# Sparse attention and a sentence-level mixture of experts on one core: program order from a list scheduler, v loaded in 96 overlapping rows, evacuations on either engine

## The chip, the core and the metric

The kernel runs on one NeuronCore of a Trainium2 chip. TensorE (PE in the profile; PEld is its weight load), VectorE (DVE), ScalarE (ACT) and GpSimd (POOL) each run their own instructions in order and wait for each other by semaphores; SyncE (SP) issues the output stores. The metric is the device time of one execution in microseconds, the median of several runs.

## What is computed

Four batch elements, each in two stages: attention over 768 positions with 8 heads of 64, then one expert out of eight, chosen for the whole element.

```python
block, window = (32, 16)
k_sum = k.reshape(B, H, nb, block, D).max(axis=3)
v_sum = v.reshape(B, H, nb, block, D).mean(axis=3)
scores_l = scale * q @ k.T          # kept where |i - j| < window, else -1e9
scores_s = scale * q @ k_sum.T + log(block)
a = softmax(concat([scores_l, scores_s]))
x = a @ concat([v, v_sum])          # heads side by side: [B, 768, 512]
...
logits = x.mean(axis=1) @ w_gate    # one row of 8 for each element
e = argmax(logits)
out = softmax(logits)[e] * (relu(x @ w1[e]) @ w2[e])   # w1: 512 x 1024, w2: 1024 x 512
```

So each query sees the 31 positions around it and 24 block summaries.

## The kernel before

**Attention tiles.** Heads go in pairs (`pr`, four of them), queries in 12 blocks of 64 (`QB`), six blocks (`u`, 0 or 1) to a score tile. A query block needs 64 own keys, 16 on each side (the halo) and 24 summaries: 120 rows. `kaugs` holds these for k, transposed, and `vblks` for v, by rows. In both the own 64 rows come first, then 16 before, 16 behind, then 24 summaries. Batch elements use two of each in turn.

**Steps of a batch element.** `T_k` and `T_q` transpose one pair of k or q (16 transposes, L252) into PSUM; `copy_on` (L261 on ACT, L263 on DVE) puts them into `kaug` and `qT`. For k the engine is fixed by batch and pair, for q it is ACT. `K_rest` takes the block maximum (`kmx`, L282, read from PSUM) and fills the halos and summaries of `kaug` (L288, L291, L294), all on DVE. `S_tile` adds the mask by matmuls (L357), then the scores (L369), and ACT takes the exp (L379). `V_sum` (L307) sums v by blocks with the matrix `bind`, `V_copy` (L322) spreads the sums over `vblk`. `O_tile` (L393) multiplies by v and DVE divides by the row sum (L401, L404). `X_tile` transposes the result (L420) and ACT writes `xT` with its sum over positions (L421). `gate` (L434 to L474) computes the logits, reads the chosen expert into a GpSimd register and issues the six weight loads (L460, L463).

**Steps of the expert.** `H_chunk`: four matmuls of 384 columns (L498), relu on DVE where `ft` and `u` are odd, else on ACT (L507, L509). `O_chunk`: half of an output tile, four matmuls of 512 columns (L521); after the second half the tile is scaled by ACT or DVE in turn (L536, L531) and stored by SP (L537).

**What sets the order.** Program order is written out by hand and each engine keeps it. `a0` lists batch 0's attention pair by pair. Then `scores(1)` runs, and from there `weave` puts scores and values of batch b+1 between H and O chunks of batch b. GpSimd's queue holds all loads: batch 0's k and q by pairs with three v loads (64 own rows L104, halos L115 and L121) behind each, index patterns for the masks in between, then batch 1, and each later batch behind the weights of an earlier one. `warm` puts matmuls on a zero tile (`zb`, L240): nine of 512 columns at the start and two of 384 before the first score tile and the first output tile of each pair of batch 0.

**PSUM.** `sc` has two buffers of two banks for scores, `one` four of one bank for everything else.

Of the kernel before, what the change touches and what calls it, by code (L numbers as in the profile page):

```python
# [18 lines left out]
AX = mybir.AxisListType  # L19


@with_exitstack
def kernel(
# [23 lines left out]
    R_PRE = QB  # L47
    R_POST = QB + HALO
# [17 lines left out]
    ld = ctx.enter_context(tc.tile_pool(name="ld", bufs=3))  # L66
    work = ctx.enter_context(tc.tile_pool(name="work", bufs=3))
    apool = ctx.enter_context(tc.tile_pool(name="ap", bufs=9))
    small = ctx.enter_context(tc.tile_pool(name="small", bufs=3))
# [4 lines left out]
    sc_pool = ctx.enter_context(tc.tile_pool(name="sc", bufs=2, space=bass.MemoryType.PSUM))  # L74
    one_pool = ctx.enter_context(tc.tile_pool(name="one", bufs=4, space=bass.MemoryType.PSUM))
# [20 lines left out]
    def load_k(b, h0=0, h1=H):  # L96
        load_rows(b, "k", k, h0, h1)

    def load_q(b, h0=0, h1=H):
        load_rows(b, "q", q, h0, h1)  # L100

    def load_v(b, h0, h1):
        vb = vblks[b % NV]
        nc.gpsimd.dma_start(  # L104
            vb[0:QB, h0:h1, :, 0:D].rearrange("p h j d -> p (h j) d"),
            v[b, h0:h1].rearrange("h (j p) d -> p (h j) d", p=QB),
        )

    def load_halos(b, h0=0, h1=H):

        vb = vblks[b % NV].rearrange("p h j d -> p (h j) d")
        rows = v[b].rearrange("h s d -> (h s) d")
        n0, n1 = h0 * NJ, h1 * NJ
        a, z = max(n0, 1), min(n1, H * NJ - 1)
        nc.gpsimd.dma_start(  # L115
            vb[R_PRE : R_PRE + HALO, a:n1, 0:D],
            rows[(a - 1) * QB : (n1 - 1) * QB].rearrange("(n p) d -> p n d", p=QB)[
                QB - HALO : QB
            ],
        )  # L120
        nc.gpsimd.dma_start(  # L121
            vb[R_POST : R_POST + HALO, n0:z, 0:D],
            rows[(n0 + 1) * QB : (z + 1) * QB].rearrange("(n p) d -> p n d", p=QB)[
                0:HALO
            ],
        )

    def load_vp(b, pr):
        load_v(b, 2 * pr, 2 * pr + 2)
        load_halos(b, 2 * pr, 2 * pr + 2)  # L130

    def clear_ends(i, eng):

        eng.memset(vblks[i][QB:R_SUM, 0:1, 0:1, 0:D], 0.0)
        eng.memset(vblks[i][QB:R_SUM, H - 1 : H, NJ - 1 : NJ, 0:D], 0.0)
# [4 lines left out]
    load_k(0, 0, 2)  # L140
    clear_ends(0, nc.vector)
    identb = const.tile([128, 128], BF16, name="identb")
    make_identity(nc, identb)
    load_q(0, 0, 2)
    load_k(0, 2, 4)
    load_q(0, 2, 4)
    load_vp(0, 0)
    it_b = const.tile([QB, NJ, BLK], I32, name="it_b")
    nc.gpsimd.iota(it_b, pattern=[[-2, NJ], [1, BLK]], base=0, channel_multiplier=0)
    it_p = const.tile([128, 1], I32, name="it_p")  # L150
    nc.gpsimd.iota(it_p, pattern=[[0, 1]], base=0, channel_multiplier=1)

    it_m = const.tile([128, R_SUM], I32, name="it_m")
    nc.gpsimd.iota(it_m[:, 0:R_PRE], pattern=[[1, QB]], base=0, channel_multiplier=-1)
    nc.gpsimd.iota(
        it_m[:, R_PRE:R_POST], pattern=[[1, HALO]], base=-HALO, channel_multiplier=-1
    )
    nc.gpsimd.iota(
        it_m[:, R_POST:R_SUM], pattern=[[1, HALO]], base=QB, channel_multiplier=-1
    )  # L160
    load_vp(0, 1)
    load_k(0, 4, 6)
    load_q(0, 4, 6)
    load_vp(0, 2)
    load_k(0, 6, 8)
    load_q(0, 6, 8)
    load_vp(0, 3)

    def load_vs(b):
        load_v(b, 0, 4)  # L170
        load_v(b, 4, 8)
        load_halos(b)

    def load_all(b):
        load_k(b)
        load_q(b)
        load_vs(b)

    wg_sb = const.tile([128, NDT, E], FP32, name="wg_sb")
    nc.sync.dma_start(wg_sb, moe_w_gate.rearrange("(g p) e -> p g e", p=128))  # L180

    def edges(i, eng):

        eng.memset(vblks[i][0:QB, :, :, D:DP], 1.0)
        eng.memset(vblks[i][R_SUM:NR, :, :, D:DP], float(BLK))
        eng.memset(vblks[i][QB:R_SUM, :, :, D:DP], 1.0)
        eng.memset(kaugs[i][:, :, 0:1, R_PRE:R_POST], 0.0)
        eng.memset(kaugs[i][:, :, NJ - 1 : NJ, R_POST:R_SUM], 0.0)
        eng.memset(kaugs[i][:, :, :, NR:128], 0.0)

    edges(0, nc.vector)
    ones_row = const.tile([1, 128], FP32, name="ones_row")
    nc.vector.memset(ones_row, 1.0)
    ident6 = const.tile([128, NW, QB], BF16, name="ident6")
    for hh in range(2):
        rs = slice(hh * D, (hh + 1) * D)
        nc.vector.tensor_copy(
            ident6[rs], identb[rs, rs].unsqueeze(1).to_broadcast([QB, NW, QB])
        )
    pf = const.tile([128, 1], FP32, name="pf")  # L200
    nc.vector.tensor_copy(pf, it_p)
    half_id = const.tile([QB, 1], FP32, name="half_id")
    nc.vector.tensor_scalar(
        out=half_id, in0=pf[0:QB, :], scalar1=float(BLK), scalar2=None, op0=ALU.is_ge
    )
    bind = const.tile([QB, NJ, BLK], BF16, name="bind")
    nc.vector.tensor_scalar(
        out=bind, in0=it_b, scalar1=half_id[:, 0:1], scalar2=None, op0=ALU.is_equal
    )
    hi64 = const.tile([128, 1], FP32, name="hi64")  # L210
    nc.vector.tensor_scalar(
        out=hi64, in0=pf, scalar1=float(QB), scalar2=float(QB),
        op0=ALU.is_ge, op1=ALU.mult,
    )
    d_f = const.tile([128, R_SUM], FP32, name="d_f")
    nc.vector.tensor_scalar(
        out=d_f, in0=it_m, scalar1=hi64[:, 0:1], scalar2=None, op0=ALU.add
    )
    nc.vector.tensor_tensor(out=d_f, in0=d_f, in1=d_f, op=ALU.mult)

    mbias = const.tile([128, 128], BF16, name="mbias")
    nc.vector.memset(mbias[:, R_SUM:128], 0.0)
    nc.vector.tensor_scalar(
        out=mbias[:, 0:R_SUM], in0=d_f, scalar1=float(HALO * HALO), scalar2=OFF,
        op0=ALU.is_ge, op1=ALU.mult,
    )


    ends = []
    for i, c0 in enumerate((R_PRE, R_POST)):  # L230
        t = const.tile([128, 128], BF16, name=f"mb_end{i}")
        nc.vector.tensor_copy(t, mbias)
        nc.vector.memset(t[:, c0 : c0 + HALO], OFF)
        ends.append(t)

    def warm(ps, n, cols=384):


        for _ in range(n):
            nc.tensor.matmul(  # L240
                ps[:, 0:cols], lhsT=zb[:, 0:128], rhs=zb[:, 0:cols], start=True, stop=True
            )


    xT, red, qTs, xss, aTs = {}, {}, {}, {}, {}

    def transpose_pair(b, which, pr, name):
        src = nat[which, b]
        ps = one_pool.tile([128, RR, PR], BF16, name=name, tag="one")
        for r in range(RR):  # L250
            for hh in range(2):
                nc.tensor.transpose(  # L252
                    ps[hh * D : (hh + 1) * D, r, :],
# [24 lines left out]
    def K_rest(b, pr):  # L278
        def f():
# [16 lines left out]
            )  # L296
        return f

    vss = {}

    def V_sum(b, prs):
        def f():
# [357 lines left out]
```

## Time and profile before

| | |
|---|---|
| three runs | 182.45, 183.06, 184.3 us; median 183.06 |
| profiled execution | 183.01 us, its span 181.4 us |
| mean granted TensorE clock | 0.925 |
| data read from HBM, written | 38.78 MB, 6.29 MB |

The span is the time from the first to the last instruction of the profiled execution; the rest of its time lies around it. The columns of a group are its line, engine, operation and tiles, the count, the busy time and mean length of one, and the idle time of the engine just before it with what ended most of it:

```profile
L379 ACT ACTIVATE aT<-sc 128x768 bf16<-128x768 f32 x32 | 25.4, 813 | 15.7 <-PE sc L369 15.7
L509 ACT ACTIVATE hT<-hps 128x384 bf16<-128x384 f32 x48 | 23.7, 493 | 17.7 <-PE hps L498 17.2
L421 ACT ACTIVATE xT<-xps 128x384 bf16<-128x384 bf16 x32 | 15.6, 492 | 11.1 <-PE xps L420 10.4
L404 DVE TENSOR_TENSOR xs<-ops,rv 128x384 bf16<-128x384 f32 x32 | 17.8, 557 | 1.1
L282 DVE TENSOR_REDUCE kmx<-kps 128x24 bf16<-128x768 bf16 x16 | 15.2, 948 | 4.9 <-ACT kaug L261 4.8
L104 POOL DMA_DIRECT2D vblk<-in_v_dram x10 | 12.3, 1235 | 1.0 <-DMA vblk<-in_v_dram 1.0
```

On DVE and ACT the last figure is large where the engine waits for PE. A mean can mix forms: a v load of L104 lasted from 968 to 1414 ns on POOL, by its rows. The loads by number, KB of each and median us from issue to landing:

```profile
w_sb<-in_moe_w_dram POOLq DMA_DIRECT2D x12, 512.0 KB, 12.4
k_nat<-in_k_dram POOLq DMA_DIRECT2D x3, 768.0 KB, 14.9
vblk<-in_v_dram POOLq DMA_DIRECT2D x6, 384.0 KB, 21.5
w_sb<-in_moe_w_dram POOLq DMA_DIRECT2D x8, 128.0 KB, 5.0
```

### The profile page before, as it was taken

To read this page: it belongs to the slowest core of one execution; us is meant where nothing else is said; L and a number is where in the kernel's file an instruction comes from. 1 tells how busy PE (TensorE), PEld (TensorE's weight loads), DVE (VectorE), ACT (ScalarE), POOL (GpSimd) and SP (SyncE) were. 2 spreads that over 40 slices of the span, in tenths; PEclk is the share of its full clock that TensorE was granted. 3 is DMA by queue.
4 is the path that set the end of the run, shared out by engine and by line. 5 is a ranking of instruction groups with operands and counts; after the bars stand their busy time and mean duration, and the time that the engine had idled before them with its cause. 6 is when DMAs were issued, how large, how long until landed. Compare 5 with 4: busy or idle time off the path is not lost.

```text
span 181.4 us, 5192 instructions
## 1 busy us (share of the span) xinstructions
PE 159.2 (88%) x2229; PEld 93.8 (52%) x2241; DVE 90.9 (50%) x241; ACT 91.5 (50%) x187; POOL 53.4 (29%) x81
## 2 busy tenths in 40 slices
PE   7467997669996978999998999999979999999990
PEld 2245765447653554455554564455646544565440
DVE  4345476766417753476638752686287522122111
ACT  2243388457972743366663762666736821454120
POOL 7979980038910003982000007200000054000000
PEclk9855579975699999999999999999999999999999
DMA  4999999999999999999999996999400019995232
GB/s 46 143 159 155 125 185 192 128 90 135 196 198 208 167 125 65 110 232 252 235 231 182 126 61 86 148 234 255 102 0 4 0 16 181 260 260 98 87 144 116
DMA packets 60166, 26.02 MB, mean 143 GB/s; under 512 B 42736, under 2 KB 57072, under 8 KB 60144
## 3 DMA queue, kind: packets, MB, share of 16 engines
q0 software_dynamic: 56160, 19.39, 145.5%
q1 hardware_dynamic: 3984, 6.31, 10.1%
q8 instruction: 17, 0.28, 0.8%
q14 instruction: 5, 0.04, 0.1%
HBM read 38.78 MB, written 6.29 MB: 249 GB/s over the span
## 4 chain that ended last, share of the span: by engine, by line
PE 76%; DVE 12%; ACT 4%; POOL 3%; issue 3%; POOLq 0%; DVEq 0%
PE o_ps L521 23%; PE hps L498 22%; PE ops L393 5%; PE sc L369 4%; PE sc L357 4%; PE kps L252 4%; PE qps L252 4%; PE vsps L307 3%; PE xps L420 3%; DVE vblk L322 2%; DVE xs L404 2%; ACT xT L421 2%; DVE kmx L282 2%; PE ops L240 1%; ACT kaug L261 1%
## 5 line engine op out<-in xcount | busy, mean ns | idle before, releaser
L498 PE MATMUL hps<-xT,w_sb 128*128 128x384 bf16 x256 | 48.8, 328 | 0.0
L521 PE MATMUL o_ps<-w_sb,hT 128*128 128x512 bf16 x180 | 42.5, 380 | 1.5 <-issue 1.3
L460 POOL DMA_DIRECT2D w_sb<-in_moe_w_dram x16 | 12.1, 765 | 91.3 <-DVE gcol L484 58.4
L379 ACT ACTIVATE aT<-sc 128x768 bf16<-128x768 f32 x32 | 25.4, 813 | 15.7 <-PE sc L369 15.7
L509 ACT ACTIVATE hT<-hps 128x384 bf16<-128x384 f32 x48 | 23.7, 493 | 17.7 <-PE hps L498 17.2
L498 PEld LDWEIGHTS <-w_sb 128*128 128x128 bf16 x256 | 22.4, 98 | 13.1 <-issue 0.2
L521 PEld LDWEIGHTS <-hT 128*128 128x128 bf16 x192 | 17.3, 98 | 19.3
L531 DVE TENSOR_SCALAR o_sb<-o_ps,gcol 128x512 f32<-128x512 f32 x12 | 9.0, 751 | 25.2 <-PE o_ps L521 22.3
L421 ACT ACTIVATE xT<-xps 128x384 bf16<-128x384 bf16 x32 | 15.6, 492 | 11.1 <-PE xps L420 10.4
L404 DVE TENSOR_TENSOR xs<-ops,rv 128x384 bf16<-128x384 f32 x32 | 17.8, 557 | 1.1
L507 DVE TENSOR_SCALAR hT<-hps 128x384 bf16<-128x384 f32 x16 | 8.9, 558 | 18.0 <-PE hps L498 17.1
L282 DVE TENSOR_REDUCE kmx<-kps 128x24 bf16<-128x768 bf16 x16 | 15.2, 948 | 4.9 <-ACT kaug L261 4.8
L536 ACT ACTIVATE o_sb<-o_ps,gcol 128x512 f32<-128x512 f32 x12 | 8.3, 688 | 18.4 <-PE o_ps L521 18.3
L261 ACT COPY qT<-qps 128x768 bf16<-128x768 bf16 x16 | 12.8, 797 | 8.1 <-PE qps L252 8.0
L369 PE MATMUL sc<-qT,kaug 64*128 64x64 bf16 x384 | 12.5, 203 | 4.3 <-DVE kaug L294 4.3
L393 PEld LDWEIGHTS <-aT 120*64 120x64 bf16 x384 | 8.9, 113 | 13.5 <-DVE vblk L322 7.1
L393 PE MATMUL ops<-vblk,aT 120*64 120x65 bf16 x384 | 11.5, 201 | 4.8 <-DVE vblk L322 4.7
L369 PEld LDWEIGHTS <-kaug 64*128 64x128 bf16 x384 | 9.3, 104 | 7.4 <-issue 4.4
L263 DVE COPY kaug<-kps 128x768 bf16<-128x768 bf16 x10 | 9.5, 951 | 6.2 <-PE kps L252 6.2
L104 POOL DMA_DIRECT2D vblk<-in_v_dram x10 | 12.3, 1235 | 1.0 <-DMA vblk<-in_v_dram 1.0
L252 PE MATMUL qps<-identb,q_nat 96*64 96x96 bf16 x256 | 10.4, 236 | 2.0 <-DMA q_nat<-in_q_dram 2.0
L401 DVE RECIPROCAL rv<-ops 128x6 f32<-128x6 f32 x32 | 6.2, 193 | 11.9 <-PE ops L393 11.9
(81 smaller groups left out, 178.1 us busy)
## 6 DMA issues: line engine op xcount, KB each, us to landing
w_sb<-in_moe_w_dram POOLq DMA_DIRECT2D x12, 512.0 KB, 12.4
out_dram<-o_sb SPq DMA_DIRECT2D x24, 256.0 KB, 6.0
k_nat<-in_k_dram POOLq DMA_DIRECT2D x3, 768.0 KB, 14.9
q_nat<-in_q_dram POOLq DMA_DIRECT2D x3, 768.0 KB, 17.6
vblk<-in_v_dram POOLq DMA_DIRECT2D x6, 384.0 KB, 21.5
vblk<-in_v_dram POOLq DMA_DIRECT2D x6, 190.0 KB, 24.2
w_sb<-in_moe_w_dram POOLq DMA_DIRECT2D x8, 128.0 KB, 5.0
w_sb<-in_moe_w_dram POOLq DMA_DIRECT2D x4, 256.0 KB, 6.7
```

Of the source, the lines that this page charges most:

```text
L104: nc.gpsimd.dma_start(vb[0:QB, h0:h1, :, 0:D].rearrange("p h j d -> p (h j) d"), v[b, h0:h1].rearrange("h (j p) d -> p (h j) d", p=QB),)
L252: nc.tensor.transpose(ps[hh * D : (hh + 1) * D, r, :], src[:, 2 * pr + hh, r * D : (r + 1) * D], identb[0:PR, 0:PR],)
L261: nc.scalar.copy(out_, in_)
L282: nc.vector.tensor_reduce(out=kmx, in_=kpss.pop((b, pr)).rearrange("q r (n p) -> q n r p", n=NB), axis=AX.XY, op=ALU.max,)
L369: nc.tensor.matmul(sc[:, hh, w * QB : (w + 1) * QB], lhsT=ka[rs, pr, j, :], rhs=qT[rs, j * QB : (j + 1) * QB], start=False, stop=w == NW - ...
L379: nc.scalar.activation(aT, sc[:, :, 0:HB], ACT.Exp, scale=SCALE)
L393: nc.tensor.matmul(ops[w * QB : (w + 1) * QB, t, hh, :], lhsT=aT[0:NR, hh, c0 : c0 + QB], rhs=vb[0:NR, 2 * pr + hh, u * NW + 2 * t + w, 0 ...
L404: nc.vector.tensor_tensor(out=xs, in0=ops[:, :, :, 0:D], in1=rv.unsqueeze(3).to_broadcast([128, NW // 2, 2, D]), op=ALU.mult,)
L421: nc.scalar.activation(xT[b][:, pr, u * HB : (u + 1) * HB], xps, ACT.Copy, accum_out=red[b][:, pr, u : u + 1],)
L498: nc.tensor.matmul(hps[:, 0:HB], lhsT=w1_sb[:, dt, ft * 128 : (ft + 1) * 128], rhs=xT[b][:, dt, u * HB : (u + 1) * HB], start=(dt == 0), s ...
L509: nc.scalar.activation(dst, hps[:, 0:HB], ACT.Relu)
L521: nc.tensor.matmul(o_ps, lhsT=hTs[b][:, ft, st * 128 : (st + 1) * 128], rhs=w2_sb[:, ft, :], start=(ft == 0), stop=(ft == NFT - 1),)
```

## The change

Four things change together.

1. **Order.** The hand-written lists, `weave` and `run` go. Every step is split into its TensorE part and its evacuation, each becomes an `Op` with an engine, a duration, a priority, what it depends on and the PSUM or SBUF slot it takes. `Plan.solve` places them one by one: of the operations that could start within 0.03 us of the earliest, the one with the lowest priority number. The program is emitted in that order. The durations and hand-over times are constants in the code; TensorE's are taken 1.8 times as long before 24 us.
2. **Engine of an evacuation.** K and q copies, relu, output scaling and the block sums of v go to whichever of ACT and DVE would end them first in the plan. Exp and `xT` stay on ACT; `kmx`, halos, division and `V_copy` on DVE.
3. **v.** `vblk` and `kaug` now have the halo before, the own 64 rows, the halo behind in that order, so that a block's 96 rows are consecutive rows of v. One load fetches them for four heads at once, overlapping rows twice; the first block of batch 0 and the last of batch 3 have their own smaller load. `bind` has 96 rows, with zeros for the halo rows.
4. **Buffers and fillers.** `sc` has one buffer, `one` six; `ld` two, `work` and `small` four. `kmx` is read from `kaug` (SBUF), not from PSUM. Of the matmuls on `zb` only the nine at the start remain. V_sum of batch 0 runs twice for two pairs instead of four times for one.

```diff
+    def solve(self):
...
+            for op in left:
+                if any(d.end is None for d in op.deps):
+                    continue
+                r = max([d.end + self.LAT[d.eng] for d in op.deps], default=0.0)
...
+                for s in op.takes:
+                    h = hist[s.pool]
+                    if len(h) >= self.bufs[s.pool]:
+                        old = h[-self.bufs[s.pool]]
...
+                        r = max(r, max(u.end + self.LAT[u.eng] for u in old.users))
...
+                for eng, dur in op.engs:
+                    st = max(r, free.get(eng, 0.0))
+                    if eng == "pe" and st < self.slow_until:
+                        dur *= self.slow
+                    c = (st + dur, st, eng)
+                    if best is None or c < best:
+                        best = c
...
+            st, _, _, end, eng, op = min(
+                (c for c in found if c[0] <= smin + 0.03), key=lambda c: (c[1], c[2])
+            )
...
-    sc_pool = ctx.enter_context(tc.tile_pool(name="sc", bufs=2, space=bass.MemoryType.PSUM))
-    one_pool = ctx.enter_context(tc.tile_pool(name="one", bufs=4, space=bass.MemoryType.PSUM))
+    sc_pool = ctx.enter_context(tc.tile_pool(name="sc", bufs=1, space=bass.MemoryType.PSUM))
+    one_pool = ctx.enter_context(tc.tile_pool(name="one", bufs=6, space=bass.MemoryType.PSUM))
...
     def load_v(b, h0, h1):
-        vb = vblks[b % NV]
-        nc.gpsimd.dma_start(
-            vb[0:QB, h0:h1, :, 0:D].rearrange("p h j d -> p (h j) d"),
-            v[b, h0:h1].rearrange("h (j p) d -> p (h j) d", p=QB),
-        )
...
+        def cells(n0, n1, p0, p1):
+            nc.gpsimd.dma_start(
+                vb[p0:p1, n0:n1, 0:D],
+                bass.AP(
+                    v.tensor,
+                    v.offset + ((b * H * NJ + n0) * QB - HALO + p0) * D,
+                    [[D, p1 - p0], [QB * D, n1 - n0], [1, D]],
+                ),
+            )
...
+    def K_max(b, pr):
+        def f(eng):
+            kmxs[b, pr] = small.tile([128, NB], BF16, name="kmx")
+            nc.vector.tensor_reduce(
+                out=kmxs[b, pr].rearrange("q (j c) -> q j c", c=QB // BLK),
+                in_=kaugs[b % 2][:, pr, :, R_OWN:R_POST].rearrange(
+                    "q j (c t) -> q j c t", t=BLK
+                ),
...
-            if b == 0 and u == 0:
-                warm(sc[:, 0], 2)
...
-            if b == 0 and u == 0:
-                warm(ops.rearrange("p t h c -> p (t h c)"), 2)
...
+    plan = Plan(
+        {"one": 6, "sc": 1, "aT": 9, "qT": 4, "xs": 4, "hT": 2, "xT": 2, "o_sb": 4,
+         "w": 2},
+        slow_until=24.0, slow=1.8,
+    )
+    EITHER = lambda a, d: [("act", a), ("dve", d)]
...
+            own = add(EITHER(0.86, 1.0), K_own(b, pr), w, [tk] + wk)
+            kmx = add(("dve", 1.0), K_max(b, pr), w, [own])
+            rest = add(("dve", 0.6), K_rest(b, pr), w - 1, [own, kmx, R["edge", b % 2]])
...
+                s = R["S", b, pr, u] = add(
+                    ("pe", 0.4), S_mm(b, pr, u), w - 10, [rest, qo, R["mask"]], [ss])
+                e = R["e", b, pr, u] = add(
+                    ("act", 0.87), S_exp(b, pr, u), w - 10, [s], [at])
...
+                m = add(("pe", 0.66), H_mm(b, ft, u), base + ft,
+                        [R["w1", b, ft]] + [R["x", b, p, u] for p in ALLP], [sl])
+                o = add(EITHER(0.55, 0.6), H_out(b, ft, u), base - 165, [m],
...
+    ORDER = ["kq1", "v1", "w0", "kq2", "v2", "w1", "kq3", "v3", "w2", "w3"]
+    loads_kq(0, "k", [0], 0.8, KQ)
+    R["ident"] = add(("pool", 1.7), constants, 0, [last[0]])
...
+    for pr in ALLP:
+        if pr:
+            loads_kq(0, "k", [pr], 0.7, KQ)
+        loads_kq(0, "q", [pr], 0.7, KQ)
+        if pr == 1:
+            loads_v(0, [0, 1], 2.2, VV)
+    loads_v(0, [2, 3], 2.2, VV)
...
+    plan.solve()
+    plan.emit()
```

The order that the plan emits, where it differs most (each name a step for one pair; the number in front is the batch):

- Batch 0's k and q of the first two pairs are transposed first, then come the score tiles. Before batch 0's gate, TensorE also has all eight transposed pairs of batch 1 and its first two score tiles. After the gate come four more score tiles with V_sum of batch 1 among them, then the first w1 chunk of batch 0, six output tiles of batch 1 in a row, its last two score tiles and its `xT` transposes, and then the other w1 chunks.
- The eight transposed pairs of batch 2 stand within and behind batch 0's w1 chunks, its score tiles between batch 0's output halves. Batch 3 has the same places in batch 1.
- Output tiles of the expert come in twos: first half of both, then second half of both.
- GpSimd: k of pair 0, `identb`, three index patterns, q of pair 0, k and q of pair 1, v of pairs 0 and 1 (two loads), k and q of pairs 2 and 3, v of pairs 2 and 3, then batch 1 as before with two v loads.
- ScalarE gets nearly all relu and output scaling of the expert.

## The prediction

> **What bounds the kernel now.** I read the page first, then the busy time by stretches of the span, then TensorE's timeline and the list of waits. The page:
>
> ```profile
> span 181.4 us, 5192 instructions
> ...
> PE 159.2 (88%) x2229; PEld 93.8 (52%) x2241; DVE 90.9 (50%) x241; ACT 91.5 (50%) x187; POOL 53.4 (29%) x81
> ...
> PE   7467997669996978999998999999979999999990
> ...
> PEclk9855579975699999999999999999999999999999
> ...
> PE 76%; DVE 12%; ACT 4%; POOL 3%; issue 3%; POOLq 0%; DVEq 0%
> ```
>
> TensorE (PE) is busy 88% and is 76% of the chain that ended last; ScalarE and VectorE are at 50%. The digits say that this isn't one regime: PE reaches 9 and stays there only from the middle of the span, and PEclk has two holes on the left. Cut at those places (columns: length, then busy us and instruction count of PE, PEld, DVE, ACT, POOL, then granted clock, DMA share, GB/s):
>
> ```profile
> 8.00:24.80 16.80, 14.41 (x210) 9.79 (x210) 8.95 (x30) 7.55 (x12) 14.98 (x26) 0.50 1.69 149
> 24.80:38.40 13.60, 10.36 (x266) 7.53 (x264) 8.94 (x27) 8.43 (x22) 1.55 (x2) 1.00 2.93 159
> 38.40:48.60 10.20, 9.21 (x188) 7.00 (x182) 6.73 (x18) 8.05 (x11) 8.61 (x10) 0.50 2.43 140
> 48.60:70.78 22.18, 18.83 (x297) 11.33 (x296) 11.38 (x34) 12.82 (x34) 2.03 (x3) 1.00 2.70 162
> 41.90:45.30 3.40, 3.40 (x72) 2.62 (x70) 1.73 (x2) 2.62 (x5) 2.73 (x5) 0.50 1.75 152
> ```
>
> ```profile
> 70.78:108.25 37.47, 35.41 (x550) 20.38 (x555) 22.73 (x52) 20.90 (x43) 10.59 (x12) 1.00 2.15 176
> 108.25:145.52 37.27, 35.24 (x551) 20.39 (x556) 22.20 (x56) 21.29 (x45) 4.51 (x6) 1.00 0.57 101
> 145.52:181.40 35.88, 31.59 (x161) 15.78 (x162) 7.41 (x17) 10.41 (x20) 4.45 (x6) 1.00 0.66 147
> ```
>
> From 70.78 (the first w2 matmul of batch 0) on, PE runs at clock 1.00 with 2.1 us idle in each of two periods (37.47 − 35.41, 37.27 − 35.24) and 4.3 in the last stretch, most of it the final store. Before 70.78, 27 us run at clock 0.50 (first and third row), and PE idles 2.4 + 3.2 + 1.0 + 3.4 us in these rows. So the first 71 us decide. Prices of one step, from PE's timeline:
>
> ```profile
> 42.68 0.85 PE L252 MATMUL kps<-identb,k_nat 96*64 96x96 bf16 x16
> 43.46 0.45 PE L357 MATMUL sc<-ident,mbias 64*128 64x320 bf16 x2
> 12.63 1.46 PE L307 MATMUL vsps<-vblk,bind 64*32 64x128 bf16 x12
> 53.34 0.85 PE L307 MATMUL vsps<-vblk,bind 64*32 64x128 bf16 x48
> 48.07 1.08 PE L498 MATMUL hps<-xT,w_sb 128*128 128x384 bf16 x4
> 57.70 0.38 PE L393 MATMUL ops<-vblk,aT 120*64 120x65 bf16 x12 [1.20 <-DVE vblk L322]
> ```
>
> A step costs the distance between starts. At clock 0.50/1.00: a transposed pair T 0.78/0.40; a score tile S (bias and kaug matmuls, 43.46 to 44.21) 0.75/0.45; an output tile O 0.40/0.31; its transposes X 0.38/0.18; V_sum of one pair 1.39/0.77; a w1 chunk H 1.3/0.65; half a w2 tile Y 0.85 at full clock.
>
> ```profile
> PE ops L393 <- DVE vblk L322: 4.7, 8, 1.2
> PE sc L369 <- DVE kaug L294: 4.3, 4, 1.4
> PE qps L252 <- DMA q_nat<-in_q_dram: 2.0, 1, 2.0
> ```
>
> These three are most of PE's waits, nearly all before 71 us.
>
> **The change, part by part.**
>
> *Loads and POOL's queue.* three iotas (0.75 us; five took from 6.85 to 7.69) move ahead of the second load, so q's first piece is issued 0.8 us later than at 2.79; it landed at 7.9 and PE waited 2.0 us for it, so the first q transposes start at about 8.5. v in 96 rows: a 1536-row piece cost POOL 0.97 us, a 3072-row piece 1.36, a 384-row piece 0.60, hence 1.8 for 4512 rows (estimate on that line). Batch 0's twelve v issues (about 9 us) become three (4.3), so batch 1's k is issued near 16 instead of 20.3. Nothing else on that queue changes places except that pairs 2 and 3 of k and q follow v directly. The bytes are the same; at the 149 GB/s of the 8 to 24.8 row the pair-0-and-1 v (0.58 MB after 0.77 MB of k and q, from 4 us) lands near 13, needed at 15: no wait. I take the v load for 0 on the path; bounds −1 (batch 1's v out of the way of the first weights sooner) to +3 (one 4512-row load that lands late blocks V_sum and all of PE behind it).
>
> *V_sum of batch 0* goes from four calls of 12 matmuls to two of 24 on two column groups. The 12-form and the 48-form both take 0.8 at full clock, so 24 take 0.8/1.4: two calls saved, 2.8 us at half clock. *Filler matmuls* on zb (two per first score tile and first output tile, 16 in all) go: 0.75 per pair of them at half clock, 0.43 at full, 4.8 us. They lie on PE, partly inside waits.
>
> *Order of batch 0 and 1.* On PE, batch 1's eight T and two S now stand before batch 0's gate. Sum from 8.5 at half clock: 15 T 11.7, 10 S 7.5, 2 V 2.8, 8 O 3.2, 8 X 3.0, gate 0.9: 29.1. Waits: the first S now stands behind two kmx in DVE's queue (kmx 0.95, copy 0.95: S near 12.7, 1.9 idle after the last T), the second S behind the exp of the first (0.85, one score buffer), the first O of pair 2 (1.0: V_copy stands behind kmx and rest): 3.9. The gate ends at 41.5; before it ended at 37.2, but without 7.7 us of T and S. Net 3.4 us ahead.
>
> *Gate to first H.* POOL took 2.2 us from the gate to the first weight issue (37.17 to 39.33), a 128 KB piece 5.7 to land in the list of transfers of 40 to 48: 49.4. Under it lie four S and V_sum of batch 1; with one score buffer an S follows the last by 0.75 + 0.81 exp + two hand-overs of 0.1, 1.75 us: to 48.4. H waits 1.0. Before, it started at 48.07 without wait.
>
> *First H to first Y.* At full clock 16 H 10.4, 8 O 2.5, 8 X 1.5, 2 S 0.9, gate 0.9: 16.2; drawn forward from batch 2: 8 T and one S, 3.65. Half-clock surcharge 2.5 (below), one O waits 0.5 for an exp behind four X evacuations. Y begins at 72.2; less the 3.65 ahead, 68.6 against 70.8: **2.2 us gained**.
>
> *Steady periods.* V_copy waits 0.23 + 0.69 and the gate's 0.28 go: 1.2 in each of two periods. (Five gaps of 0.16 put down to issue stand where a Y shows x3 for x4: a record is missing, nothing to gain.) New: an S after only one Y waits, 1.75 − 0.3 (faster S) − 0.45 − 0.85 = 0.15 and more if its exp is late; 0.25 taken, twice: 0.5. **1.9 gained**. Evacuations: ACT gets most of H and Y (0.49 and 0.69 against 0.56 and 0.75), per batch 8 exp 6.5, 8 X about 4.8, 13 H 6.5, Y 3.8, copies 4: 26 of 36 us, so ACT still has cover; the k copy with its separate kmx moves nothing on DVE (0.95 each as now, now in series after ACT's copy, which kmx already followed: kmx waited 4.8 us for it).
>
> kmx now reads SBUF; nearest row 948 ns, bounds 0.8 to 1.1, hidden beside Y in the steady part. Buffers: `ld` falls from three to two, but batch 2's k and q then reuse batch 0's tiles, whose transposes end some 20 us before that issue; `one` grows from four to six. *SP and the end.* Stores stay 24 and in order, but Y tiles come in twos, so the last two stores start 0.85 apart instead of 1.7, both evacuated by ACT: 256 KB lasts about 1.3 us at some 200 GB/s (estimate from the rates of the rows), **0.3 lost**. H to Y at the end is as before.
>
> Sum: 2.2 + 1.9 − 0.3 = 3.8; span 177.6. The profiled run took 183.01 for a span of 181.4, so 1.6 lies around it; its time equals the median 183.06. **179.2 us.**
>
> **A rule against the rows.** In 41.90 to 45.30 PE is busy 3.40 of 3.40 us with T and S and the clock is 0.50; it came at 48.6, after the first H. The Trainium skill (TensorE: Matmul & The Clock Gate, Part 1) says that one busy window of about 3.4 us releases the clock: then the changed kernel, dense from 17 us, would run its first two batches at full clock, and the sum would be 171.5 (B below). The same page, Part 4: PE-mode transpose, says that a transpose doesn't count as busy in the same way, which is what the row shows, and that speaks against this change: it takes out the zb matmuls, of which a pair runs at 23.7, just ahead of the clock's rise at 24.8, and puts eight transposes more in that stretch. I take the row: half clock until H. By it the surcharge after the first H is between 0.6 us of half clock (as at 48.07) and all of the O, S, X and four H that follow (5.3); 2.5 is nearer the row.
>
> **The rivals.**
>
> *A, the sum above*, 0.42, alone 176 to 182.5.
>
> *B, the clock rises near 24.8 as it does now*, 0.18. Then from there to the gate 8 T, 6 S, 4 O, 6 X and the gate save 6.7, of which 1.5 comes back as exposed evacuations: gate at 36.3, weights 44.2, no surcharge: 64.5 at the first Y, less 3.65: 9.9 gained instead of 2.2: 171.5. For: dense PE. Against: the 41.9 row.
>
> *C, it doesn't do what it says*: clock late (surcharge 5.3) and the score waits eat the steady gain: −0.6 + 0 − 0.3: 183.9; 0.18.
>
> *D, slower: the scores chain themselves to ScalarE.* `sc` has one buffer for two. Each S waits on PE until ACT has taken the last exp, and ACT takes it in a fixed order behind relu, X and copies that the planner placed with its own durations; everything behind S on PE waits too. PE's list of waits now names no exp. 24 tiles in batches 1 to 3: 0.35 us each is 8.4: 187.6. It decides from (3.8 + 1.8)/24 = 0.23 us per tile. For: `aT <- sc` is ACT's largest row (25.4 us). Against: two Y halves between S's in most places give 1.7 us. 0.22.
>
> **Numbers.** One per cent, what a measurement of this kernel can tell from no change, is 1.8 us: faster is under 181.2, slower over 184.9. A lies under 181.2 four times in five: 0.34, with B 0.18 and a little of C: 0.56. Within 1%: the rest of A and most of C, 0.20. Slower: D and C's tail, 0.24. The range 172 to 187 leaves out part of B below and part of D above.
>
> **What would show it.** Right: granted clock 0.50 from about 8 to 50 us; gate of batch 0 near 41; first H near 49 after a short DMA wait; first Y near 72 with eight transposed pairs of batch 2 done; no V_copy wait from there. Wrong: clock 1.00 in the thirties (B); PE waiting for exp by more than 6 us in all (D); PE waiting for vblk's DMA at 13 to 16 us.

## The result and the profile after

| | before | after |
|---|---|---|
| median of four runs | 183.68 us | 174.12 us (173.73 to 175.92) |
| ratio to before | 1 | 0.9458, 95% interval 0.9378 to 0.9539 |
| profiled execution, its span | 183.01, 181.4 us | 175.92, 174.2 us |

The gain is 9.6 us by the medians; 3.8 were predicted. Two more executions of the changed kernel took 172.88 and 178.79 us. Ratios and intervals leave out executions more than 1.5% above the fastest of their kernel, medians do not, and the profiled execution of the changed kernel is such a one, at a mean clock of 0.901 (0.905 to 0.921 in the other three). The page of the changed kernel:

```profile
PE 151.6 (87%) x2214; PEld 93.2 (53%) x2225; DVE 83.1 (48%) x224; ACT 100.9 (58%) x204; POOL 45.9 (26%) x62
...
PE   6627887495857999989999999999999999999990
...
PEclk9965589855597599999999999999999999999999
```

TensorE is still the bound, 87% busy, but with 7.6 us less of work (159.2 before, the fillers among it), and the holes in PEclk are still there. (Before its first recorded change, here at 6.45 us, PEclk reads full clock, though a transposed pair at 5.28 takes 0.85 us, as at half clock.) The same stretches as before, then the stretch from the first w2 matmul of batch 0 to that of batch 2 in each kernel (columns as in the prediction):

```profile
8.00:24.80 16.80, 11.73 (x266) 9.44 (x267) 12.64 (x25) 8.44 (x16) 10.44 (x14) 0.59 1.78 174
24.80:38.40 13.60, 9.92 (x271) 8.03 (x270) 10.11 (x26) 10.12 (x20) 0.00 (x0) 0.83 2.30 145
38.40:48.60 10.20, 7.92 (x196) 5.87 (x197) 4.61 (x18) 6.25 (x12) 6.16 (x9) 0.56 0.58 64
48.60:70.78 22.18, 19.17 (x238) 11.49 (x233) 12.44 (x32) 12.85 (x34) 7.92 (x8) 0.85 1.89 181
73.58:138.35 64.77, 63.16 (x962) 37.81 (x965) 34.46 (x93) 43.60 (x93) 9.76 (x11) 1.00 1.08 156
138.35:174.20 35.85, 31.61 (x161) 15.75 (x162) 0.87 (x3) 15.15 (x28) 4.10 (x6) 0.99 0.67 147
```

```profile
70.78:145.51 74.73, 70.64 (x1100) 40.76 (x1109) 44.92 (x107) 42.19 (x88) 15.10 (x18) 1.00 1.36 139
```

The first three rows have clocks of 0.56 to 0.83, so no full clock from the twenties on, but no steady 0.50 either. The decisive pair of rows is 74.73 against 64.77 us. Of these 9.96 us, 3.65 are work that now stands ahead of the stretch (eight transposed pairs and a score tile, priced in the prediction; in the trace they take 3.66 from their starts to the next ones); **6.3 us are gained where 1.9 were predicted**. Idle time of PE in it falls from 4.09 (74.73 − 70.64) to 1.61: 2.5 us. Its busy time falls by 7.48, so 3.8 more than the moved work. That TensorE would need less time for the same steps isn't in the prediction at all. The last stretch (35.85 against 35.88) gained and lost nothing.

The waits of TensorE after (us in total, times, longest):

```profile
PE sc L411 <- ACT aT L438: 3.2, 4, 0.9
PE xps L482 <- DVE xs L469: 2.9, 5, 1.6
PE sc L423 <- DVE kaug L347: 2.9, 1, 2.9
```

The waits for `vblk` and `kaug` that led this list before (4.7 and 4.3) are down to one of 0.5 and one of 2.9, at 13.09. Score tiles wait for ScalarE in four places, at 14.49 and from 40.56 to 44.00, and an output tile waits for it once more, 1.4 us. What replaced them is seen in the timeline. First before, then after, both a few us behind the first w2 matmul:

```profile
76.97 0.53 PE L252 MATMUL kps<-identb,k_nat 96*64 96x96 bf16 x16
77.43 1.04 PE L521 MATMUL o_ps<-w_sb,hT 128*128 128x512 bf16 x4
78.40 0.31 PE L357 MATMUL sc<-ident,mbias 64*128 64x320 bf16 x2
...
78.77 0.35 PE L369 MATMUL sc<-qT,kaug 64*128 64x64 bf16 x12
79.05 0.53 PE L252 MATMUL qps<-identb,q_nat 96*64 96x96 bf16 x16
```

```profile
76.66 1.90 PE L617 MATMUL o_ps<-w_sb,hT 128*128 128x512 bf16 x8
78.50 0.31 PE L411 MATMUL sc<-ident,mbias 64*128 64x320 bf16 x2
...
78.67 0.34 PE L423 MATMUL sc<-qT,kaug 64*128 64x64 bf16 x12
78.94 1.90 PE L617 MATMUL o_ps<-w_sb,hT 128*128 128x512 bf16 x7
...
85.26 1.14 PE L452 MATMUL ops<-vblk,aT 120*64 120x65 bf16 x60
86.33 0.31 PE L411 MATMUL sc<-ident,mbias 64*128 64x320 bf16 x2
```

Before, half a w2 tile (`o_ps` x4), a transposed pair, half a tile, a score tile and again a pair follow each other. After, two halves (x8, a record missing in the second row) stand together between score tiles, with no transposed pair, and five output tiles of the attention (`ops` x60) take 1.07 us to the next start, 0.21 each; the prediction's price of one alone was 0.31.

### The profile page after: what moved, and what is told of

Read it like the earlier page. It is cut to its first block, busy times and chain, and to the rows that moved or that the text cites. A ratio compares the mean times of both kernels' runs of the same rounds, so it can differ in the third digit from the quotient of the medians.

```text
span 174.2 us, 5138 instructions
## 1 busy us (share of the span) xinstructions
PE 151.6 (87%) x2214; PEld 93.2 (53%) x2225; DVE 83.1 (48%) x224; ACT 100.9 (58%) x204; POOL 45.9 (26%) x62
## 4 chain that ended last, share of the span: by engine, by line
PE 77%; DVE 12%; ACT 4%; issue 4%; POOL 1%; DVEq 0%; POOLq 0%; ACTq 0%
PE hps L589 25%; PE o_ps L617 24%; PE tps L300 7%; PE sc L411 5%; PE ops L452 4%; PE xps L482 4%; DVE vblk L390 4%; PE sc L423 4%; PE vsps L369 3%; ACT aT L438 3%; DVE xs L469 2%; DVE kmx L328 1%; DVE bind L286 1%; DVE kaug L341 1%; PE lgps L505 1%
## 5 line engine op out<-in xcount | busy, mean ns | idle before, releaser
L589 PEld LDWEIGHTS <-w_sb 128*128 128x128 bf16 x256 | 24.4, 101 | 15.9 <-issue 1.5
L608 ACT ACTIVATE hT<-hps 128x384 bf16<-128x384 f32 x53 | 25.2, 492 | 12.7 <-PE hps L589 12.6
L636 ACT ACTIVATE o_sb<-o_ps,gcol 128x512 f32<-128x512 f32 x21 | 14.4, 687 | 17.4 <-PE o_ps L617 12.7
L188 POOL DMA_DIRECT2D vblk<-in_v_dram x10 | 15.7, 1576 | 0.5 <-DMA vblk<-in_v_dram 0.5
L606 DVE TENSOR_SCALAR hT<-hps 128x384 bf16<-128x384 f32 x11 | 6.1, 558 | 19.7 <-PE hps L589 19.5
L328 DVE TENSOR_REDUCE kmx<-kaug 128x24 bf16<-128x768 bf16 x16 | 15.0, 947 | 0.9 <-ACT kaug L310 0.9
L411 PE MATMUL sc<-ident,mbias 64*128 64x320 bf16 x64 | 11.2, 346 | 3.3 <-ACT aT L438 3.2
L390 DVE COPY vblk<-vs_sb 24x1536 bf16<-24x1536 bf16 x16 | 11.8, 735 | 4.2 <-ACT vs_sb L310 3.7
L482 PE MATMUL xps<-identb,xs 128*128 128x128 bf16 x96 | 11.1, 245 | 2.9 <-DVE xs L469 2.9
L310 ACT COPY kaug<-tps 128x768 bf16<-128x768 bf16 x11 | 8.8, 799 | 6.3 <-PE tps L300 6.3
L300 PE MATMUL tps<-identb,q_nat 96*64 96x96 bf16 x256 | 8.9, 230 | 3.4 <-issue 2.2
```

The lines of the kernel that those rows point to most:

```text
L300: nc.tensor.transpose(ps[hh * D : (hh + 1) * D, r, :], src[:, 2 * pr + hh, r * D : (r + 1) * D], identb[0:PR, 0:PR],)
L328: nc.vector.tensor_reduce(out=kmxs[b, pr].rearrange("q (j c) -> q j c", c=QB // BLK), in_=kaugs[b % 2][:, pr, :, R_OWN:R_POST].rearrange(" ...
L390: nc.vector.tensor_copy(vblks[b % NV][R_SUM:NR, 2 * pr : 2 * pr + 2, :, 0:D], vss[b, pr][BLK * pr : BLK * pr + NB] .unsqueeze(2) .to_broad ...
L411: nc.tensor.matmul(sc[:, hh, cs], lhsT=bias[rs, :], rhs=ident6[rs].rearrange("p w c -> p (w c)")[:, cs], start=i == 0, stop=False, tile_po ...
L482: nc.tensor.transpose(xps[:, t * 128 : (t + 1) * 128], xs[:, t], identb)
L589: nc.tensor.matmul(hps[:, 0:HB], lhsT=w1_sb[:, dt, ft * 128 : (ft + 1) * 128], rhs=xT[b][:, dt, u * HB : (u + 1) * HB], start=(dt == 0), s ...
```

## Experiments

### Does the price of a step depend on its neighbour?

Theory 1: TensorE pays about 0.1 us where a matmul of 128 rows and 128 columns of weights (w1 chunk H, w2 half Y) stands beside one of a smaller form (output tile O of 120 x 64, score tile S of 64 rows). Rival, theory 2: it doesn't, and the gain is waits and buffers. First a probe behind the whole program of the changed kernel, on data that are in place by then:

```diff
     plan.emit()
...
+        seg([h], 12)
+        seg([o], 12)
+        seg([xx], 12)
+        seg([y], 8)
+        seg([h, o], 12)
+        seg([h, xx], 12)
+        seg([h, h, o, o], 6)
+        seg([h, h, h, h, o, o, o, o], 3)
...
+    probe()
```

> The changed kernel with a probe behind its last step: on TensorE alone, at full clock, w1 chunks (H), output tiles (O), xT transposes (X), w2 halves (Y) and score tiles (S) in runs of one kind, then alternating. Theory 1 (a step costs more when its neighbour is of another kind): H and O in runs 0.65 and 0.21 us, alternating some 1.06 a pair, 0.2 more than in runs; in twos half of that, in fours a quarter. Theory 2 (TensorE's work is the same in any order and only waits were removed): all four arrangements within 0.02 us a pair.

The timeline of its TensorE:

```profile
168.28 7.96 PE L871 MATMUL prba<-xT,w_sb 128*128 128x384 bf16 x48
176.18 2.47 PE L887 MATMUL prbb<-vblk,kaug 120*64 120x65 bf16 x144
...
198.16 0.82 PE L871 MATMUL prbe<-xT,w_sb 128*128 128x384 bf16 x4
198.91 0.38 PE L887 MATMUL prbe<-vblk,kaug 120*64 120x65 bf16 x12
199.23 0.82 PE L871 MATMUL prbe<-xT,w_sb 128*128 128x384 bf16 x4
...
208.48 0.81 PE L871 MATMUL prbf<-xT,w_sb 128*128 128x384 bf16 x4
...
209.30 0.81 PE L871 MATMUL prbf<-xT,w_sb 128*128 128x384 bf16 x4
```

Twelve H in a row take 7.90 to the next start (0.658 each), twelve O 2.40 (0.200). Alternating, H and O together take 1.07 (198.16 to 199.23) where 0.86 would be the sum: 0.1 for each change. In twos a pair took 0.952, in fours 0.897. H beside the 128 x 128 transposes X costs nothing (208.48 to 209.30: 0.82, and 0.658 and 0.168 are 0.826). Y and S, alternating further on, take 1.42 for a pair (236.10 to 237.52), against 0.86 and 0.34 in runs: 0.11 for each change. So it is the change of form that costs, not that of the step. Which part of the form matters, the rows or the columns of the weights, was not tested.

That was outside the kernel. In place, every H chunk of the changed kernel got one more matmul in its middle, of 65 columns of zeros into columns that nobody reads, once in the form of O (shown) and once in the form of H (`hps[:, 384:449]`, `zb[:, 0:128]`, `zb[:, 0:65]`):

```diff
                     stop=(dt == NDT - 1),
                 )
+                if dt == 1:
+                    nc.tensor.matmul(
+                        hps[0:64, 384:449], lhsT=zb[0:120, 0:64], rhs=zb[0:120, 0:65],
+                        start=False, stop=False,
+                    )
```

> The changed kernel with one matmul more in the middle of every H chunk (64 of them), of the form of an output tile (120 rows, 64 columns of weights, 65 of data, zeros), into columns that nothing reads. Theory 1 (a step pays about 0.1 us for each change of form beside it, in the kernel as in the probe): two changes more per chunk, so H stretches by about 0.03 + 0.2 us; 64 chunks give 13 to 15 us, of which at most 2 fall into waits: 186 to 188 us, and H in the stretch of two periods grows from 0.65 to about 0.88 each. Theory 2 (inside the kernel the neighbour costs nothing, and H was shorter after the change for another reason): like the control, 176 to 177.

> Control: the same extra matmul in each H chunk, with the same 65 columns, but in the form of H itself (128 rows, 128 columns of weights). Both theories: 0.03 to 0.05 us each, 2 to 3 us in all, 176 to 177. The difference to the other run is the price of the change of form alone.

Measured: 187.44 us (ratio 1.0129, 1.0010 to 1.0248) in the form of O, 176.18 us (0.9521, 0.9439 to 0.9602) in the form of H. The timelines of the two, first the form of O:

```profile
98.34 0.82 PE L589 MATMUL hps<-xT,w_sb 128*128 128x384 bf16 x4
99.09 0.22 PE L597 MATMUL hps<-zb 120*64 120x65 bf16 x1
99.24 0.82 PE L589 MATMUL hps<-xT,w_sb 128*128 128x384 bf16 x4
```

```profile
98.85 0.82 PE L589 MATMUL hps<-xT,w_sb 128*128 128x384 bf16 x4
99.50 0.19 PE L597 MATMUL hps<-zb 128*128 128x65 bf16 x1
99.53 0.82 PE L589 MATMUL hps<-xT,w_sb 128*128 128x384 bf16 x4
```

From one H start to the next it is 0.90 us with two changes of form and 0.68 without: 0.11 per change, as expected. Over the kernel it is 11.3 us for 128 changes by the medians, 0.09 each, and 10.3 us, 0.08 each, by those executions that the ratios count (186.0 against 175.7). Theory 1 holds inside the kernel; theory 2 would have had the two equal.

The next kernel has the longer runs of like steps without the rest of the change. It is the hand-written order of before with coarser weaving: three w1 chunks, then the output tiles due by then, and two w2 halves between the score steps.

```diff
-            want = (m * (i + 1)) // n
+            want = (m * (i + 1)) // n if (i + 1) % g == 0 or i + 1 == n else done
...
-            weave(os_[b - 1][4:12] + hs[b][0:2], scores(b + 1))
+            weave(os_[b - 1][4:12] + hs[b][0:2], scores(b + 1), 2)
...
-            weave(hs[b][4:16], values(b + 1))
+            weave(hs[b][4:16], values(b + 1), 3)
```

> Before, with the weaving in batches 1 to 3 made coarser: w1 chunks in threes between values, w2 halves in twos between scores. Theory 1: fewer changes of kind, TensorE's busy time in the two steady periods falls by 1 us each, some of it given back in waits: 181 to 182.5. Theory 2: busy time unchanged, waits the same or more: 183 to 185.

191.81 us, ratio 1.0418 (1.0322 to 1.0514): slower, which neither theory's figure allows for. The changes of form in the two periods fell from 76 to 48 and the 32 H chunks from 23.4 to 21.8 us by distance of starts, but TensorE's busy time did not fall by the 2 us expected (70.6 before, 71.7 here), and its idle time went from 4.1 to 8.6. The wait that leads the list of the whole run:

```profile
PE sc L369 <- DVE kaug L294: 6.6, 6, 1.5
```

`kaug` is at 6.6 where before had 4.3, and the granted clock dropped in the second period (0.96 there), which lengthens the work. So here the runs did not pay: what they saved is seen in H above all, and waits and clock took more than that.

### Order, or the split of PSUM?

Four cells: hand-written order or the plan's, each with two score buffers and four others (as before) or one and six. The two in the upper row, `v_alone` and `hand_sc1`, take the new v rows with their loads and `kmx` from SBUF, and keep the order (the part of the kernel from `a0` on), the fixed engines, the fillers and the SBUF buffers of before. `plan_sc2_pool` is the changed kernel, in its order, with the pools below; in `after_sc2` the planner is given these numbers too.

```diff
-    sc_pool = ctx.enter_context(tc.tile_pool(name="sc", bufs=1, space=bass.MemoryType.PSUM))
-    one_pool = ctx.enter_context(tc.tile_pool(name="one", bufs=6, space=bass.MemoryType.PSUM))
+    sc_pool = ctx.enter_context(tc.tile_pool(name="sc", bufs=2, space=bass.MemoryType.PSUM))
+    one_pool = ctx.enter_context(tc.tile_pool(name="one", bufs=4, space=bass.MemoryType.PSUM))
...
-        {"one": 6, "sc": 1, "aT": 9, "qT": 4, "xs": 4, "hT": 2, "xT": 2, "o_sb": 4,
+        {"one": 4, "sc": 2, "aT": 9, "qT": 4, "xs": 4, "hT": 2, "xT": 2, "o_sb": 4,
```

> The hand-written order, fixed engines, fillers and buffers of before, with the v load in 96 rows, the new row order and kmx from SBUF alone. Theories 1 and 2: the gain is in the order, so this stays within 1.5 us of before (183). Rival (the v load carries it: fewer issues on GpSimd, earlier batch 1): 178 or less.

> The hand-written order, engines and fillers of before on the new v rows, but with the PSUM split of the change (one score buffer, six others). If the order carries the gain: 181 to 186, since the hand order has score tiles close together. If the split carries it without the planner: 178 or less.

> The changed kernel's order, planned for one score buffer and six others, run with two and four. If the order alone carries it: within 1.5 us of 174. If the order needs the six buffers: output and transpose tiles in runs wait for their evacuations, 178 to 184.

> The changed kernel with the PSUM split of before (two score buffers, four others), planned for it. If the single score buffer costs what TensorE waits for exp (3.2 us in the profile after): 171 to 173. If the six others carry the gain: 176 to 179. If neither matters: within 1.5 us of 174.

| ratio to before | two score buffers, four others | one score buffer, six others |
|---|---|---|
| hand-written order | 1.0005 (0.9949 to 1.0061) | 1.0669 (1.0530 to 1.0807) |
| order of the plan | 0.9877 (0.9747 to 1.0007) | 0.9458 (0.9378 to 0.9539) |

Planned for the old split, it is 0.9826 (0.9719 to 0.9933). The v rows with their single load and `kmx` from SBUF are together worth nothing that can be measured; the two were not parted, and waits for `kaug` rose from 4.3 to 8.7 us. In the hand-written order the split loses 11 us (195.33 against 184.4 in those executions of `v_alone` that its ratio counts). The order with the old split gains 1 to 2% (one of the two intervals reaches 1), and only both together give the result. The waits say something of why; `hand_sc1`, then `after_sc2`:

```profile
PE sc L419 <- ACT aT L446: 5.9, 8, 0.9
```

```profile
PE xps L482 <- DVE xs L469: 6.1, 19, 0.4
```

In the hand-written order two score tiles follow each other within one step, and with one buffer the second waits for the exp of the first eight times, 5.9 us: that is rival D of the prediction. The rest of the 11 us isn't named by the waits (those for `kaug` are 7.4 us, no more than the 8.7 in `v_alone`). The plan puts two w2 halves between most score tiles, and there no score tile waits for the exp. With four other buffers instead of six, X waits for the division 19 times, 6.1 us, against five times and 2.9. In the changed kernel's own order on the old split (`plan_sc2_pool`) the changes of form in the two periods are as many as in the changed kernel, 44, but TensorE idles 4.9 us there instead of 1.6: what the six buffers take away is waits.

### Engines and fillers

The changed order with the fixed engines of before for K, q, relu, output and block sums (each comment names the step):

```diff
+            eng = "act" if b == 0 or b == 1 and pr % 2 else "dve"   # K_own
+            eng = "act"                                             # Q_all
+            eng = "dve"                                             # V_out
-            if eng == "dve":    # H_out
+            if ft % 2 and u:
-            if eng == "dve":    # Y_out
+            if st % 2:
```

> The changed kernel's order with the engines of before for k, q, relu, output scaling and block sums. If the choice of engine matters: 177 or more (ScalarE has slack only because the planner spread the work). If TensorE is the bound and either engine keeps up: within 1.5 us of 174.

174.44 us, 0.9543 (0.9430 to 0.9656): no difference to the changed kernel that can be measured. Evacuations on either engine are not where the gain is.

The sixteen matmuls on `zb` put back before the first score tile and first output tile of each pair of batch 0:

```diff
+            if b == 0 and u == 0:
+                warm(sc[:, 0], 2)
...
+            if b == 0 and u == 0:
+                warm(ops.rearrange("p t h c -> p (t h c)"), 2)
```

> The changed kernel with the sixteen zb matmuls of before put back before the first score and output tile of each pair of batch 0. If they bring the clock up and keep it up: early part at 1.00 from about 25 to 47 us, 170 to 172. If they only cost TensorE time: 175 to 178. If neither: within 1 us of 174.

175.15 us, 0.9585 (0.9466 to 0.9705): the intervals overlap, so their removal, 1 us by the medians, can't be told from nothing. They don't hold the clock up: 0.50 from 38.4 to 48.6 in that run.

### The early part

The first score tile of the changed kernel waits 2.93 us, to 13.09, for the last copy into its `kaug` (lines in the last section). There are three edits of the plan, in four combinations, and one of the load. The first hunks are `after_lat0`; `pr == 2` comes with `..._vlate`, `slow_until=48.0` with `..._slow48`, and the last hunk is `after_v3`:

```diff
-                r = max([d.end + self.LAT[d.eng] for d in op.deps], default=0.0)
-                ok = True
+                ok, held = True, 0.0
...
-                        r = max(r, max(u.end + self.LAT[u.eng] for u in old.users))
+                        held = max(held, max(u.end + self.LAT[u.eng] for u in old.users))
...
-                    st = max(r, free.get(eng, 0.0))
+                    r = max(
+                        [d.end + (self.LAT[d.eng] if d.eng != eng else 0.0) for d in op.deps],
+                        default=0.0,
+                    )
+                    st = max(r, held, free.get(eng, 0.0))
...
-        if pr == 1:
+        if pr == 2:
             loads_v(0, [0, 1], 2.2, VV)
...
-        slow_until=24.0, slow=1.8,
+        slow_until=48.0, slow=1.8,
...
-        cells(n0, n1, 0, R_SUM)
+        cells(n0, n1, R_OWN, R_POST)
+        cells(n0, n1, 0, R_OWN)
+        cells(n0, n1, R_POST, R_SUM)
```

> The changed kernel with one change in its planner: no hand-over time between two operations on the same engine, so that the first pair's halo copies stand before the second pair's kmx on VectorE. First score tile after its bias some 1 to 2 us earlier than at 13.1 us. If the start sets the end: 172 to 173. If the early part waits for something else (weights, clock): within 1 us of 174.

> As the run before, with v of pairs 0 and 1 issued after k and q of pair 2, so that the long v issue on GpSimd comes later. If VectorE's halo copies are slow because GpSimd issues v at that time (1.55 us instead of 0.2 at 10.5 us): those copies 0.2 us, but V_sum waits for v; 173 to 175. If the copies are slow for another reason: still over 1 us.

> As the first, with TensorE planned slow until 48 us instead of 24, nearer to the granted clock of the profile. If the planner's wrong clock costs waits: 170 to 172. If an order planned for half clock leaves TensorE more idle: 175 or more.

> The two planner edits that each gained in the first batches, together: no hand-over time on the same engine with v of pairs 0 and 1 issued behind k and q of pair 2, and TensorE taken 1.8 times as long before 48 us in place of 24. Theory: they act on different stretches (v before 20 us, the order of batch 0 and 1 after it), so most of both gains add: 170 to 171. Rival: both only fill the same half-clock stretch: 172, as the first alone.

> The changed kernel with v in three loads (64 own rows, 16 before, 16 behind) for the same rows. If v by one load is worth something: GpSimd's issues for v nearly double, 175.5 or more. If it is worth nothing, as in the hand-written order: within 1 us of 174.

| | median us | ratio to before | interval |
|---|---|---|---|
| after_lat0: no hand-over time in the plan on the same engine | 174.46 | 0.9459 | 0.9399 to 0.9518 |
| after_lat0_vlate: and v of pairs 0, 1 behind k, q of pair 2 | 172.14 | 0.9296 | 0.9235 to 0.9356 |
| after_lat0_slow48: lat0, and TensorE slow in the plan to 48 us | 172.89 | 0.9384 | 0.9334 to 0.9434 |
| after_both: all three | 174.02 | 0.9409 | 0.9335 to 0.9482 |
| after_v3: v in three loads again, order of the change | 176.06 | 0.9537 | 0.9469 to 0.9605 |

`after_lat0` starts scores earlier, at 10.77, but then waits 2.0 us for v's DMA; with v issued later (`after_lat0_vlate`) that wait is 0.6, and the gate starts at 35.55 instead of 38.69 (39.52 in the changed kernel). This is the fastest kernel measured; its interval lies below that of the changed kernel (each against before). Why the late v gains is not shown beyond these times. The other edits don't add to it: together they came out at 174.02, within the interval of `after_lat0`, so the rival's 172 was missed as well as the theory's 170 to 171. Three loads instead of one give 4.3 us of waits for v in two places, but the interval overlaps with that of the changed kernel; whether the one load matters is open.

## Why the prediction was too small

**The step that failed** is the sum of the steady periods: "1.2 in each of two periods", less 0.5 for new score waits, "**1.9 gained**". The stretch gained 6.3. The idle term was near: 1.9 predicted, 2.5 measured. The missing term is TensorE's own time. The sum took each step at one price and so held the 35.4 us of busy time per period fixed, and it fell by 3.8 over the two. From PE's timeline, changes between the large forms (H, Y, X, gate) and the smaller ones (O, S, T, V) fall from 76 to 44 in that stretch (two matmuls of one row at each gate left out). At the measured 0.08 to 0.11 us, 32 changes are 2.6 to 3.5 us of the 3.8. The steps show the same: by distance of starts, waits left out, an H chunk went from 0.73 to 0.68 on average, an O tile from 0.31 to 0.25 and a transposed pair from 0.47 to 0.40, with 0.66 and 0.20 the prices of H and O in runs. For 32 H, 16 O and the 8 pairs that stayed this is some 3.3 us; the rest isn't attributed. The prediction had read O's 0.31 off single tiles between H chunks: most of two changes was in it. The Trainium skill (TensorEngine Tiling (Array Packing), Key Properties) says that changing the tiling mode drains TensorE; it gives no figure, and this case's price is 0.08 to 0.11 us. The price may be this drain; no run here shows that. The prediction did not weigh it.

**First H to first Y, and all before it** (2.2 predicted): the first Y of the profiled run starts at 73.58, predicted 72.2; less 3.65 it is 69.9 against 70.8, 0.9 gained. In `after_oldeng`, with the same order and a higher clock from 48.6 on (0.94 to 66 us, against 0.80), it starts at 70.16: 4.3 gained. By the medians 9.6 − 6.3 leaves about 3. The step was right in sign, and right in size within what the clock varies from run to run. Inside it sizes were off and cancelled in part, which is luck. The gate ended at 40.1 rather than 41.5, and the first H came at 46.91 without a wait rather than at 49.4. But from there to the first Y it took 26.7 us instead of 22.8. X waited for the division five times, 2.9 us, all before 55.2, where one wait of 0.5 was priced. And half clock came back from 54.24 to 61.06:

```profile
50.82:54.23 3.41, 1.74 (x28) 1.04 (x28) 3.17 (x11) 2.04 (x8) 1.22 (x1) 1.00 1.16 184
54.24:57.65 3.41, 3.04 (x35) 1.85 (x36) 2.12 (x7) 1.99 (x7) 0.00 (x0) 0.50 1.24 207
57.65:61.06 3.41, 3.41 (x16) 1.95 (x15) 0.34 (x1) 1.47 (x5) 0.00 (x0) 0.50 1.25 208
```

In the lower two rows PE is busy 6.45 us at half clock, so some 3.2 are lost (an estimate: half of it); with what half clock there is before 47.41, that is over the 2.5 allowed.

**Loads and v:** the first S was at 13.09 for a predicted 12.7 (part of that by a stretched copy that was not foreseen, see below), V_sum didn't wait for its load, and v with `kmx` from SBUF was worth 0 (`v_alone` 1.0005): right. **Fillers:** 4.8 us of work, "partly inside waits": 1 us by the medians, so mostly inside them. **Engines:** that ACT has cover held. **The end:** 0.3 lost was predicted, nothing was lost.

**Rivals.** B, full clock from the twenties on, didn't happen, though its 171.5 is nearer to the result than the sum: near by luck, for the unforeseen gain lay in the steady stretch. `after_both` came close to B's condition, with full clock from 20.43 to 37.50 and a gate that ended at 33.4. Its first Y still came at 71.14 (B: 64.5): waits of 4.0 and 3.3 us came after the gate, and TensorE ran at 0.50 for 13.7 of the 17.1 us from 37.50 on. What B left out is that the clock falls back when TensorE waits. The prediction's reason against B doesn't hold either: a stretch of transposes and score tiles alone did release the clock in `v_alone` (last section), and 0.50 throughout was too strict. C fell. D, scores chained to ScalarE by the single buffer, is real: it shows in `hand_sc1` at 195.33. In the plan's order the waits for exp are four of score tiles and one of an output tile, 4.6 us in all, under the 6 that the prediction named as its mark. The split was costed as a risk alone; what six other buffers save in waits was not costed.

## What to carry to other kernels

Where TensorE is the bound, price a step by its neighbours: count the changes between full 128 x 128 matmuls and smaller forms and give each 0.1 us, before pricing any wait. Runs of like steps need buffers for as many results, and inputs that are ready as early; order and buffers are one decision, and either alone can lose (`before_runs` 4%, `hand_sc1` 7%). A wait early on can cost twice, by itself and by the half clock that followed it here. A price read off a step that stands alone has its changes of form in it.

## What the runs showed of the hardware

**VectorE's copies within SBUF can stretch while GpSimd issues a load.** The lines show a halo copy and the summary copy of `kaug` in the changed kernel, the next pair's halo copy, and GpSimd's issue of v, 1.78 us:

```profile
10.53 1.55 DVE L341 COPY kaug<-kaug 128x176 bf16<-128x176 bf16 x1
...
12.04 0.90 DVE L347 COPY kaug<-kmx 128x288 bf16<-128x288 bf16 x1
12.86 0.14 DVE L341 COPY kaug<-kaug 128x176 bf16<-128x176 bf16 x1
```

```profile
10.26 1.78 POOL L188 DMA_DIRECT2D vblk<-in_v_dram  x1
```

The first copy takes 1.55 us for a median of 0.199 and ends at 12.07, with the issue (12.04); the same copy of the next pair, at 12.86, takes 0.14. `V_copy` has a median of 0.556 and a longest of 1.735, which starts at 17.62 within an issue and ends at 19.35, after that issue (19.00). Not every copy beside an issue is stretched: the `V_copy` just before, at 17.04, took 0.56, and in `after_v3`, where v's issue runs from 11.18 to 12.60, copies at 11.33 and 11.45 took 0.20 and 0.18, and only the next was stretched, to the issue's end:

```profile
11.56 1.08 DVE L349 COPY kaug<-kmx 128x288 bf16<-128x288 bf16 x1
```

The block-maximum that stands before them, from 9.65 on, isn't stretched (0.95, as ever). The Trainium skill (Advanced Engine Details and Errata, VectorE Performance Modes) says that VectorE's second port to SBUF is shared with GpSimd, and that VectorE's instructions in the modes with two ports and GpSimd's block each other; the trace agrees for the bf16 copies that were held. The run meant to test it, `after_lat0_vlate`, didn't: other issues stood beside its copies, which took 0.64 and 0.69 rather than the 0.2 expected. The first score tile starts at 11.55 in `after_v3`, whose first pair's copies took 0.2 to 0.3, so of the wait to 13.09 some 1.5 us are the stretch (an estimate); most of the rest is the second pair's block-maximum, 0.95 us, which stands ahead of the copies.

**The clock follows how busy TensorE was just before.** In the profiles of all 17 runs the granted clock changes at multiples of 3.41 us from its first change. Leaving out that first change and the end of the program, it rises 47 times: each time TensorE had been busy for at least 3.02 of the 3.41 us before, 40 times for all of them. It falls 47 times, each time after 3.41 us with 1.03 to 2.64 us of work. The three rows in the part on the first H and the first Y show a fall at 54.24, after 1.74 us of work, and a row that was busy throughout before the rise at 61.06. This is no full rule: eight stretches that were busy throughout were not followed by a rise, the one from 41.81 in the kernel before among them, and some with as little as 1.9 us of work were not followed by a fall. A stretch with transposed pairs and score tiles alone, followed by full clock, in `v_alone`:

```profile
40.08:43.49 3.41, 3.41 (x78) 2.68 (x77) 1.67 (x5) 2.32 (x3) 3.41 (x6) 0.50 1.16 118
43.49:46.90 3.41, 2.04 (x70) 1.55 (x68) 3.35 (x6) 2.91 (x4) 3.41 (x4) 1.00 1.21 170
```

Where the steps of 3.41 us lie differs from run to run (the first change is at 6.45 in the changed kernel, at 4.41 in `after_fill`), so like work can get another clock: one order gave 0.59, 0.83, 0.56 in the three early stretches of the changed kernel and 0.59, 0.83, 0.67 in `after_oldeng`, and with fillers it was 0.70, 0.88, 0.50. No run tested this by an edit.
